# Attention, feed-forward and gated convolution in one kernel: the sign of converted float64 weights by a Prelu slope, and a weight bound from blocks multiplied with themselves

## The chip, the cores and the metric

The kernel runs on one core of a Trainium2 chip. The metric is the device time of one execution in microseconds. TensorE (PE) does matrix products, VectorE (DVE) and ScalarE (ACT) elementwise work and reductions, GpSimd (POOL) almost nothing here, and SyncE's queue (SP) issues every DMA, in order.

## The reference

Three stages follow each other. q and k are rotated by position and attention is computed for 4 batches of 8 heads, 576 positions and 64 features; the result goes through a layer norm, a relu feed-forward with a residual; then through a gated causal convolution over 5 positions.

```python
scores = scale * np.matmul(q_rot, k_rot.transpose(0, 1, 3, 2))
attn = np.exp(scores - max); attn = attn / (sum + 1e-09)
x = np.matmul(attn, v)                       # to (4, 576, 512)
xn = (x - mu) / np.sqrt(var + 1e-06) * g_ln
x = x + np.maximum(xn @ w_ch1, 0.0) @ w_ch2  # 512 -> 2048 -> 512
gate_pre += conv_w[k] * xp[:, k:k + S, :]    # k = 0..4
out = (1 / (1 + np.exp(-gate_pre)) * (x @ w_val)) @ w_out
```

The weights w_ch1 and w_ch2 (512 x 2048 and 2048 x 512), w_val, w_out (512 x 512) and conv_w arrive as float64; the rest is float32.

## The kernel before, in words

[...] A conversion handles 128 x 1024 values of w_ch1 or w_ch2 (eight groups each, w = 0 and 1), or 128 x 512 of w_val and w_out (four groups each), or the 20 columns of conv_w. Its steps are: `load` puts the raw words into one of three buffers in `wall` (w = 0) or one of two buffers `kk` (w = 1); `p1` on ScalarE takes the upper words as float32, once through Abs with a scale of 2^-112 and once through Sign into a float16 scratch; `p2` on VectorE shifts the scaled value left by 3 bits and then ors in the upper bits of the lower word; `p3` on VectorE multiplies by the sign. For w_ch1 and w_ch2 `p3` also sends two matmuls of 512 columns, with the absolute values before the sign is put on, into a PSUM tile `bound`: a sum of all the weights' absolute values by column, with |g_ln| (`gab`) or ones as the stationary side.

When all eight groups of a matrix are in, `conv_scale` reduces `bound` to its maximum and makes a power of two from it (`scl`, and `sg`, which is `scl` times g_ln). With it `conv_hi` (ScalarE) and `conv_lo` (VectorE) split each weight into two float16 halves in `wall`, for which the feed-forward's matmuls (`hp` and `acc`) wait.

This runs beside attention. Work is set into an agenda of slots, one slot for a tile of 128 query rows: scores (`sc`, TensorE), the negative maximum (`nmx`, VectorE), the exponential and a float16 high part (ScalarE), the low part (VectorE), a DMA transpose `pT` and the product with v (`ov`). The conversions of w_ch1 lie two slots apart from slot -7, those of w_ch2 two slots apart from slot 14. The feed-forward begins when the first rows are through attention and the split halves of w_ch1 are there (`w1_ready`), its second layer when those of w_ch2 are (`w2_ready`). The small matrices are converted near the end of attention (`start_tail`).

A scheduler then reorders the instructions of each engine by a timeline of its own, so the order on an engine is not that of the agenda. All loads keep their order among themselves:

```python
with tc.issue_after(last_load[-1]) if last_load else nullcontext():
    last_load.append(nc.sync.dma_start(**kw).ins)
```

A load waits on SP until its buffer is free, and the transposes that come later on SP wait behind it.

Of the kernel before, what the change touches and what calls it, by code (L numbers as in the profile page):

```python
# [7 lines left out]
F32 = mybir.dt.float32  # L8
# [23 lines left out]
def pow2_below_inverse(nc, pool, bound, name):  # L32

    m = pool.tile([128, 1], F32, name=name + "_m", tag=name + "_m", bufs=1)
    nc.vector.tensor_scalar(out=m, in0=bound, scalar1=1e-30, scalar2=1.02, op0=ALU.max, op1=ALU.mult)
    nc.vector.reciprocal(out=m, in_=m)
    r = pool.tile([128, 1], F32, name=name + "_r", tag=name + "_r", bufs=1)
    nc.vector.tensor_scalar(out=r.bitcast(I32), in0=m.bitcast(I32), scalar1=0x7F800000, scalar2=None, op0=ALU.bitwise_and)
    return r


@with_exitstack
def kernel(ctx: ExitStack, tc: tile.TileContext, qk, v, g_ln, w_ch1, w_ch2, w_val, conv_w, w_out, rope, eye, out):
# [69 lines left out]
    w1, w2 = wall[:, 0:16], wall[:, 16:32]  # L113
    wf = wall.rearrange("p u n -> p (u n)").bitcast(F32).rearrange("p (u n) -> p u n", n=512)
    scl = wpool.tile([128, 4], F32, name="scl")
    gab = wpool.tile([128, KD + 1], F32, name="gab")
    sg = wpool.tile([128, KD], F32, name="sg")
    ps_h = L(sF, "ps_h", 1, space=PSUM)
    ps_a = L(sF, "ps_a", 1, space=PSUM)
# [236 lines left out]
    def upper(x):  # L356

        return x.bitcast(BF16).rearrange("p (n two) -> p n two", two=2)[:, :, 1]

    class Conv:  # L360
# [3 lines left out]

        def __init__(self, scratch, src, out, bound=None):
            self.scratch, self.src, self.out, self.bound = scratch, src, out, bound
            self.n = out.shape[1]

        def load(self):
            raw = self.scratch[0][:, 0:2 * self.n].bitcast(I32)
            load_in_order(out=raw.rearrange("p (a n) -> p a n", a=self.src.shape[1]), in_=self.src)
            self.raw = raw.rearrange("p (n two) -> p n two", two=2)

        def p1(self):
            hf = self.raw[:, :, 1].bitcast(F32)
            self.s = self.scratch[1].bitcast(F16)[:, 0:self.n]
            nc.scalar.activation(out=self.out, in_=hf, func=ACTF.Abs, scale=F64_SCALE)
            nc.scalar.activation(out=self.s, in_=hf, func=ACTF.Sign)  # L380

        def p2(self):
            ai = self.out.bitcast(I32)
            nc.vector.tensor_scalar(out=ai, in0=ai, scalar1=3, scalar2=0x7FFFFFFF, op0=ALU.logical_shift_left, op1=ALU.bitwise_and)
            nc.vector.scalar_tensor_tensor(out=ai, in0=self.raw[:, :, 0], scalar=29, in1=ai, op0=ALU.logical_shift_right, op1=ALU.bitwise_or)  # L385

        def p3(self):
            if self.bound is not None:
                o, g, k, last = self.bound
                for j in range(2):  # L390
                    nc.tensor.matmul(o, upper(g).to_broadcast([128, 128]), upper(self.out[:, j * 512:j * 512 + 512]), start=(k == 0 and j == 0), stop=(last and j == 1))
            nc.vector.tensor_tensor(out=self.out, in0=self.out, in1=self.s, op=ALU.mult)

        def schedule(self, i, after=0):
            at(max(i - 3, count[1], after), LD, self.load)
            at(i, AC, self.p1)
            at(i + 1, DV, self.p2)
            at(i + 2, PRE, self.p3)

    wfu = wf.rearrange("p u n -> p (u n)")  # L400
    unit = lambda x, a, n: x[:, a * 512:(a + n) * 512]
    scratch = (
        ([unit(wfu, a, 4) for a in (18, 22, 26)], [unit(wfu, a, 1) for a in (30, 31, 32, 33)]),
        ([unit(k, 0, 4) for k in kk], [unit(wfu, a, 1) for a in (32, 33, 32, 33, 32, 33, 32)] + [unit(kk[0], 0, 1)]),
    )

    def conv_scale(w):
        m = wpool.tile([128, 1], F32, name=f"wm{w}")
        nc.vector.tensor_reduce(out=m, in_=bound[w], axis=AX.X, op=ALU.max)
        r = pow2_below_inverse(nc, wpool, m, f"w{w}")  # L410
        nc.vector.tensor_scalar(out=scl[:, w:w + 1], in0=r, scalar1=2.0 ** 15, scalar2=None, op0=ALU.mult)
        nc.vector.tensor_scalar(out=scl[:, 2 + w:3 + w].bitcast(I32), in0=r.bitcast(I32), scalar1=-1.0, scalar2=float(0x7F000000), op0=ALU.mult, op1=ALU.add)
        if w == 0:
            nc.vector.tensor_scalar(out=sg[:, 0:KD], in0=g_sb, scalar1=scl[:, 0:1], scalar2=None, op0=ALU.mult)
        else:
            nc.vector.tensor_scalar(out=scl[:, 2:3], in0=scl[:, 2:3], scalar1=scl[:, 3:4], scalar2=2.0 ** -30 / (XN_SCALE * H_SCALE), op0=ALU.mult, op1=ALU.mult)
# [14 lines left out]
    def schedule_w(w, a0, step, i):  # L431


        bound[w] = ps_a.tile([128, DM], F32, name=f"bound{w}", tag=f"acc{w}")
        for g in range(8):
            if w == 0:
                fb, c = divmod(g, KD)
                src = w_ch1[c * 128:(c + 1) * 128, fb * 2048:(fb + 1) * 2048].unsqueeze(1)
            else:
                src = w_ch2[g * 256:(g + 1) * 256, :].rearrange("(a p) n -> p a n", p=128)  # L440
            u = 16 * w + 2 * g + 2
            Conv([r[g % len(r)] for r in scratch[w]], src, unit(wfu, u, 2), (bound[w], gab[:, (g % KD if w == 0 else KD):][:, 0:1], g, g == 7)).schedule(int(a0 + g * step), i)
# [131 lines left out]
    def start_tail(i):  # L574
        wp = R(ctx, "w3", 1)
        tw = R(sT, "tw", 1)
        raw = [tw.tile([128, 1024], F32, name=f"r3_{j}") for j in range(4)]
        tmp = [tw.tile([128, 512], F32, name=f"t3_{j}") for j in range(7)]
        rg = (raw, tmp[0:3])
        sc3 = lambda n: [r[n % len(r)] for r in rg]  # L580
        cw = tail["cw"] = wp.tile([128, KT * KD], F32, name="cw")
        Conv(sc3(0), conv_w.unsqueeze(1), cw).schedule(i + 1)
        n = 2
        for nm, src in (("wv", w_val), ("wo", w_out)):
            hi = wp.tile([128, KD, DM], F32R, name=nm + "h")
# [220 lines left out]
```

## Time and profile before

| | |
|---|---|
| median of 3 runs | 808.23 us (802.83 to 810.99) |
| profiled execution | 807.91 us |
| its span, first to last instruction | 805.8 us |
| TensorE busy | 718.7 us, 89% |
| VectorE busy | 628.9 us, 78% |
| ScalarE busy | 499.1 us, 62% |
| mean granted TensorE clock | 0.974 |

The shares are of the whole span; the stages differ, so the rows further down are taken by stretches. An engine's busy time is the time in which one of its instructions runs; neighbours on VectorE and ScalarE overlap by about 0.1 us, so what an instruction costs its queue is read from the starts of two neighbours. The line numbers are those of the kernel before.

### The profile page before, as it was taken

How to read it: one execution, taken by the hardware profiler on the slowest of the kernel's cores; microseconds unless marked ns; L12 is line 12 of the kernel's file. 1: busy time of each engine (PE TensorE's matmuls, PEld its weight loads, DVE VectorE, ACT ScalarE, POOL GpSimd, SP SyncE). 2: the span in 40 equal slices, each digit the busy share in tenths (PEclk: the TensorE clock that was granted, in tenths of full speed). 3: DMA queues.
4: the chain of work that ended last, by engine and by line, in shares of the span. 5: the costliest groups of instructions: out<-in, count | busy, mean ns of one | idle time of the engine just before them, and what ended most of it. 6: DMA issues, size and time to landing. Idle time of an engine off the chain costs nothing.

```text
span 805.8 us, 16042 instructions
## 1 busy us (share of the span) xinstructions
PE 718.7 (89%) x6353; PEld 538.6 (67%) x6360; DVE 628.9 (78%) x1237; ACT 499.1 (62%) x998; POOL 12.5 (2%) x15
## 2 busy tenths in 40 slices
PE   2346757899999988999999999999899999999997
PEld 1124546777776766777776777776567777777996
DVE  5999999999786879677778976655889745547994
ACT  4768777798874766756766767654665333324553
POOL 0000010001000000000000000000000000000000
PEclk9999968899999998999999999999999999999999
DMA  6959776767885776848757855745744102022211
GB/s 241 322 153 279 219 212 177 152 125 163 160 187 92 144 154 122 156 109 141 155 99 150 157 134 95 99 69 97 220 96 79 41 14 53 1 53 52 54 53 53
DMA packets 225835, 103.41 MB, mean 128 GB/s; under 512 B 210528, under 2 KB 213600, under 8 KB 224736
## 3 DMA queue, kind: packets, MB, share of 16 engines
q1 hardware_dynamic: 225760, 102.39, 57.1%
q8 instruction: 50, 0.82, 0.4%
q14 instruction: 25, 0.20, 0.1%
HBM read 45.73 MB, written 4.72 MB: 63 GB/s over the span
## 4 chain that ended last, share of the span: by engine, by line
PE 68%; DVE 14%; DMA 10%; ACT 4%; issue 3%; SPq 1%; ACTq 0%; DVEq 0%
PE acc L548 20%; PE hp L513 20%; PE sc L279 9%; PE pv L649 6%; PE po L666 6%; PE ov L319 4%; DMA raw<-in_qk_dram 3%; DVE nmx L284 2%; PE ov L322 2%; DVE p L298 2%; DMA wall<-in_moe_w_ch_dram 2%; DVE raw L184 2%; DMA kk<-in_moe_w_ch_dram 1%; DMA vt<-in_v_dram 1%; DVE wall L385 1%
## 5 line engine op out<-in xcount | busy, mean ns | idle before, releaser
L513 PE MATMUL hp<-xT,wall 128*128 128x256 f16 (+1 forms) x1920 | 209.4, 266 | 2.9 <-ACT hr L528 1.3
L513 PEld LDWEIGHTS <-wall 128*128 128x128 f16 x1920 | 173.1, 100 | 33.0 <-issue 6.1
L548 PE MATMUL acc<-wall,hh 128*128 128x512 f16 x544 | 162.7, 383 | 5.5 <-DVE t L385 3.1
L291 ACT ACTIVATE p<-sc,nmx 128x576 f32<-128x576 f32 x144 | 106.0, 738 | 69.0 <-DVE nmx L284 67.9
L298 DVE SCALAR_TENSOR_TENSOR p<-p,p 128x576 f16<-128x576 f32 x144 | 107.2, 749 | 24.1 <-ACT p L293 23.5
L284 DVE TENSOR_REDUCE nmx<-sc 128x1 f32<-128x576 f32 x144 | 105.8, 748 | 15.5 <-PE sc L279 15.4
L293 ACT ACTIVATE p<-p 128x576 f16<-128x576 f32 x144 | 96.4, 682 | 18.1 <-DMA pT<-p 16.3
L548 PE MATMUL acc<-wall,hl 128*128 128x512 f16 x272 | 100.5, 381 | 0.2 <-DVE hl L535 0.2
L319 PE MATMUL ov<-vh,pT 128*128 128x64 f16 (+1 forms) x1296 | 95.0, 204 | 4.0 <-ACT vh L235 3.0
L319 PEld LDWEIGHTS <-pT 128*128 128x128 f16 x1296 | 81.4, 103 | 18.2 <-issue 9.8
L548 PEld LDWEIGHTS <-hh 128*128 128x128 f16 x544 | 49.3, 98 | 58.7 <-issue 6.5
L279 PE MATMUL sc<-kq 64*128 64x288 f32 x576 | 82.1, 312 | 5.2 <-ACT p L291 5.2
L535 DVE TENSOR_TENSOR hl<-hr,hh 128x512 f16<-128x512 f32 (+1 forms) x72 | 47.2, 655 | 47.7 <-ACT hr L528 47.6
L526 ACT ACTIVATE hh<-hp 128x512 f16<-128x512 f32 (+1 forms) x72 | 40.8, 567 | 66.5 <-PE hp L513 66.5
L279 PEld LDWEIGHTS sc<-kq 64*128 64x128 f32 x576 | 63.1, 186 | 21.3 <-issue 8.3
L322 PE MATMUL ov<-vl,pT 128*128 128x64 f16 (+1 forms) x720 | 72.7, 204 | 2.3 <-DVE vl L240 2.3
L635 DVE SCALAR_TENSOR_TENSOR gt<-xT,cw,gt 128x256 f32<-128x256 f32 (+12 forms) x192 | 69.6, 412 | 3.3 <-ACT gt L629 2.9
L184 DVE TENSOR_TENSOR raw<-raw,rope_sb 128x1152 f32<-128x1152 f32 (+2 forms) x40 | 44.3, 1111 | 25.1 <-DMA raw<-in_qk_dram 25.1
L322 PEld LDWEIGHTS <-pT 128*128 128x128 f16 x720 | 56.0, 103 | 6.6 <-issue 1.6
L279 PE MATMUL sc<-kx,qs 64*128 64x288 f32 x144 | 34.0, 400 | 24.5 <-ACT p L291 23.5
L666 PE MATMUL po<-woh,gv 128*128 128x512 f32 x144 | 48.7, 403 | 0.0
L279 PEld LDWEIGHTS sc<-kx,qs 64*128 64x128 f32 x144 | 26.8, 259 | 31.8 <-ACT p L291 29.4
(121 smaller groups left out, 1034.8 us busy)
## 6 DMA issues: line engine op xcount, KB each, us to landing
raw<-in_qk_dram SPq DMA_DIRECT2D x28, 576.0 KB, 5.5
wall<-in_moe_w_ch_dram SPq DMA_DIRECT2D x8, 1024.0 KB, 6.5
kk<-in_moe_w_ch_dram SPq DMA_DIRECT2D x8, 1024.0 KB, 6.1
vt<-in_v_dram SPq DMA_DIRECT2D x16, 320.0 KB, 3.7
out_dram<-x SPq DMA_DIRECT2D x18, 256.0 KB, 2.0
pT<-p SPq DMA_TRANSPOSE x144, 3.4
r<-in_moe_w_val_dram SPq DMA_DIRECT2D x4, 512.0 KB, 4.3
r<-in_moe_w_out_dram SPq DMA_DIRECT2D x4, 512.0 KB, 4.5
```

The lines of the kernel that those rows point to most:

```text
L184: nc.vector.tensor_tensor(out=a, in0=a, in1=t, op=ALU.mult)
L279: nc.tensor.matmul(live[i + e][:, half, 0:HS], lw[rows, a], xk[rows, k, half * HS:(half + 1) * HS], start=(n == 0), stop=(n == 2))
L284: nc.vector.tensor_reduce(out=nmx, in_=sc[:, :, 0:HS], axis=AX.XY, op=ALU.max, negate=True)
L291: nc.scalar.activation(out=p32.rearrange("p (e n) -> p e n", e=2), in_=sc[:, :, 0:HS], func=ACTF.Exp, bias=nmx, accum_out=dens[g % 5][:, j ...
L293: nc.scalar.activation(out=p16[:, 0], in_=p32, func=ACTF.Copy, scale=P_SCALE)
L298: nc.vector.scalar_tensor_tensor(out=p16[:, 1], in0=p32, scalar=P_SCALE, in1=p16[:, 0], op0=ALU.mult, op1=ALU.subtract)
L319: nc.tensor.matmul(o, pT[:, c], vh[:, hs, c, :], start=(c == 0), stop=(c == 8))
L322: nc.tensor.matmul(o, pT[:, c], vl[:, hs, c, :], start=False, stop=False)
L513: nc.tensor.matmul(hp[:, j, 0:w], w1[:, u, wl * 512 + o:wl * 512 + o + 128], xT[:, xl * KD + c, 0:w], start=(i == 0), stop=(i == 3 * KD - 1))
L548: tail["last"] = nc.tensor.matmul(st["acc"][s], lw[:, j, sl], w2[:, f + j, lo * 512:lo * 512 + 512], start=(f + j == 0 and i == 0), stop=( ...
L635: nc.vector.scalar_tensor_tensor(out=gt[:, c0:c1], in0=xT[:, c, HALO + c0 - s:HALO + c1 - s], scalar=col(KT - 1 - s), in1=gt[:, c0:c1], op ...
L666: nc.tensor.matmul(po, lw[:, d, sl], rx[:, d, :], start=(n == 0), stop=(n == 3 * KD - 1))
```

## The change

Five things are changed.

- `p1` is one activation, Prelu with the same scale and the slope -(2^32), in place of Abs and Sign. For a negative input the slope makes the result positive and raises its exponent by 32, and the shift by 3 moves that exponent bit into the sign's place. The mask of the shift in `p2` goes, so that its instruction has one operation in place of two.
- `p3` has no product any more. The float16 scratch for the signs goes.
- The bound is taken from the converted weights: for each block of 128 columns, one matmul of the block with itself, all added up in one 128 x 128 tile `bound`. Its largest value is the largest sum of squares by column. A group of 1024 values sends eight such matmuls with a weight load each in place of two of 512 columns.
- `conv_scale` takes the root by halving the exponent (`pow2_below_inverse_root`, one more VectorE instruction than before), and for w_ch1 multiplies by the square of the largest |g_ln| (`gmax`, one more).
- `gmax` is made at the start, by four matmuls of `gab` with the identity and a VectorE reduction.

```diff
+def pow2_below_inverse_root(nc, pool, bound, name):
+    m = pool.tile([128, 1], F32, name=name + "_m", tag=name + "_m", bufs=1)
+    nc.vector.tensor_scalar(out=m, in0=bound, scalar1=1e-30, scalar2=1.05, op0=ALU.max, op1=ALU.mult)
+    nc.vector.reciprocal(out=m, in_=m)
+    r = pool.tile([128, 1], F32, name=name + "_r", tag=name + "_r", bufs=1)
+    nc.vector.tensor_scalar(out=r.bitcast(I32), in0=m.bitcast(I32), scalar1=1, scalar2=0x7F800000, op0=ALU.logical_shift_right, op1=ALU.bitwise_and)
+    nc.vector.tensor_scalar(out=r, in0=r, scalar1=2.0 ** 63, scalar2=None, op0=ALU.mult)
     return r
...
         def p1(self):
-            hf = self.raw[:, :, 1].bitcast(F32)
-            self.s = self.scratch[1].bitcast(F16)[:, 0:self.n]
-            nc.scalar.activation(out=self.out, in_=hf, func=ACTF.Abs, scale=F64_SCALE)
-            nc.scalar.activation(out=self.s, in_=hf, func=ACTF.Sign)
+            nc.scalar.activation(out=self.out, in_=self.raw[:, :, 1].bitcast(F32), func=ACTF.Prelu, scale=F64_SCALE, alpha=-(2.0 ** 32))
 
         def p2(self):
             ai = self.out.bitcast(I32)
-            nc.vector.tensor_scalar(out=ai, in0=ai, scalar1=3, scalar2=0x7FFFFFFF, op0=ALU.logical_shift_left, op1=ALU.bitwise_and)
+            nc.vector.tensor_scalar(out=ai, in0=ai, scalar1=3, scalar2=None, op0=ALU.logical_shift_left)
...
         def p3(self):
-            if self.bound is not None:
-                o, g, k, last = self.bound
-                for j in range(2):
-                    nc.tensor.matmul(o, upper(g).to_broadcast([128, 128]), upper(self.out[:, j * 512:j * 512 + 512]), start=(k == 0 and j == 0), stop=(last and j == 1))
-            nc.vector.tensor_tensor(out=self.out, in0=self.out, in1=self.s, op=ALU.mult)
+            o, start, stop = self.bound
+            k = self.n // 128
+            for j in range(k):
+                x = upper(self.out[:, j * 128:j * 128 + 128])
+                nc.tensor.matmul(o, x, x, start=(start and j == 0), stop=(stop and j == k - 1))
...
         nc.vector.tensor_reduce(out=m, in_=bound[w], axis=AX.X, op=ALU.max)
-        r = pow2_below_inverse(nc, wpool, m, f"w{w}")
+        if w == 0:
+            nc.vector.tensor_scalar(out=m, in0=m, scalar1=gmax, scalar2=gmax, op0=ALU.mult, op1=ALU.mult)
+        r = pow2_below_inverse_root(nc, wpool, m, f"w{w}")
...
-        bound[w] = ps_a.tile([128, DM], F32, name=f"bound{w}", tag=f"acc{w}")
+        bound[w] = ps_a.tile([128, 128], F32, name=f"bound{w}", tag=f"acc{w}")
...
-        tmp = [tw.tile([128, 512], F32, name=f"t3_{j}") for j in range(7)]
+        tmp = [tw.tile([128, 512], F32, name=f"t3_{j}") for j in range(4)]
...
-    nc.vector.memset(gab[:, KD:KD + 1], 1.0)
-    nc.scalar.activation(out=gab[:, 0:KD], in_=g_sb, func=ACTF.Abs)
+    nc.scalar.activation(out=gab, in_=g_sb, func=ACTF.Abs)
+    gt0 = ps_h.tile([128, KD, 128], F32, name="gt0", tag="hp")
+    for c in range(KD):
+        nc.tensor.matmul(gt0[:, c], upper(gab[:, c:c + 1]).to_broadcast([128, 128]), ident, start=True, stop=True)
+    nc.vector.tensor_reduce(out=gmax, in_=gt0, axis=AX.XY, op=ALU.max)
```

In all, VectorE has 22 instructions fewer, ScalarE 25 fewer, TensorE 100 matmuls and 100 weight loads more; the DMAs are the same. The scheduler orders all of it anew. Two places follow.

VectorE in the conversion of w_ch1, around the scale of the first part of v (`vs`, `sv`), in the kernel before. L384 and L385 are the shift and the or of `p2`, L392 is the sign product, L226, L35, L38, L231 and L232 make v's scale, L188 and L206 rotate and split q, L331 belongs to the softmax sum.

```order
L226 TENSOR_REDUCE vm<-hp 128x1
L38 TENSOR_SCALAR vs_r<-vs_m 128x1
L385 SCALAR_TENSOR_TENSOR wall<-wall 128x1024
L188 TENSOR_TENSOR raw<-raw 128x128
L392 TENSOR_TENSOR wall<-wall 128x1024
L231 TENSOR_SCALAR sv<-vs_r 128x1
L232 TENSOR_SCALAR sv<-vs_r 128x1
L35 TENSOR_SCALAR vs_m<-vm 128x1
L384 TENSOR_SCALAR wall<-wall 128x1024
L392 TENSOR_TENSOR wall<-wall 128x1024
L206 SCALAR_TENSOR_TENSOR qs<-raw,qs 128x128
L331 TENSOR_SCALAR rd<-den_63,sv 128x5
```

The same place after the change; L394 and L395 are now the shift and the or, L296 the negative maximum of a score tile, L310 the low part of the probabilities, and lines 196, 243, 244 and 343 are the former 184, 231, 232 and 331.

```order
L394 TENSOR_SCALAR wall<-wall 128x1024
L36 RECIPROCAL vs_m<-vs_m 128x1
L310 SCALAR_TENSOR_TENSOR p_442<-p_440,p_442 128x576
L395 SCALAR_TENSOR_TENSOR wall<-wall 128x1024
L38 TENSOR_SCALAR vs_r<-vs_m 128x1
L296 TENSOR_REDUCE nmx<-sc 128x1 x2
L243 TENSOR_SCALAR sv<-vs_r 128x1
L244 TENSOR_SCALAR sv<-vs_r 128x1
L394 TENSOR_SCALAR wall<-wall 128x1024
L343 TENSOR_SCALAR rd<-den_63,sv 128x5
L196 TENSOR_TENSOR raw<-raw,rope_sb 128x2x128
L395 SCALAR_TENSOR_TENSOR wall<-wall 128x1024
```

Between the scale of v and the first softmax sum there stood two sign products; now only a shift stands there.

SP's queue where the loads of w_ch2 (`kk`) go out, in the kernel before. `raw` is a load of q or k, `pT` the transpose of one tile's probabilities; the numbers behind p are those of its buffers.

```order
L300 DMA_TRANSPOSE pT<-p_603 128x9x128
L66 DMA raw<-in_qk_dram 128x2x320
L66 DMA kk<-in_moe_w_ch_dram 128x2x1024 x2
L66 DMA raw<-in_qk_dram 128x2x320
L300 DMA_TRANSPOSE pT<-p_653 128x9x128
L300 DMA_TRANSPOSE pT<-p_686 128x9x128
L300 DMA_TRANSPOSE pT<-p_727 128x9x128
L66 DMA kk<-in_moe_w_ch_dram 128x2x1024
```

The same place after the change.

```order
L77 DMA kk<-in_moe_w_ch_dram 128x2x1024
L77 DMA raw<-in_qk_dram 128x2x320
L312 DMA_TRANSPOSE pT<-p_603 128x9x128
L312 DMA_TRANSPOSE pT<-p_641 128x9x128
L77 DMA kk<-in_moe_w_ch_dram 128x2x1024
L312 DMA_TRANSPOSE pT<-p_693 128x9x128
L312 DMA_TRANSPOSE pT<-p_726 128x9x128
L77 DMA kk<-in_moe_w_ch_dram 128x2x1024
```

The loads of w_ch2 stood in pairs and then three transposes; now there is one load after every two transposes.

## Rows read from the trace of the kernel before

**Rows 1.** Windows: from, to, busy time of PE, PEld, DVE, ACT, POOL (instructions), clock, DMA, GB/s

```profile
15.00:60.00 45.00, 17.79 (x93) 9.29 (x94) 42.94 (x75) 32.06 (x55) 0.00 (x0) 1.00 0.77 246
60.00:105.00 45.00, 28.59 (x201) 21.99 (x203) 43.88 (x95) 37.21 (x61) 0.00 (x0) 1.00 0.94 252
105.00:165.00 60.00, 45.63 (x510) 40.05 (x514) 57.82 (x94) 44.40 (x90) 4.42 (x2) 0.77 0.73 174
165.00:806.00 641.00, 624.52 (x5543) 465.66 (x5539) 477.73 (x960) 380.30 (x787) 7.56 (x8) 0.99 0.52 105
```

**Rows 2.** Chain of waits from 0 to 200 us, shares of that stretch by line

```profile
by line: PE sc L279 10.6%; issue 6.9%; DMA wall<-in_moe_w_ch_dram 6.8%; PE acc L548 6.5%; PE hp L513 6.0%; DMA kk<-in_moe_w_ch_dram 5.7%; PE ov L319 4.8%; DVE wall L385 4.7%; DVE wall L392 4.2%; DVE raw L184 4.0%; DMA raw<-in_qk_dram 4.0%; 
```

**Rows 3.** Chain of waits, pieces from 92 to 127 us: start, length, what

```profile
93.67 5.73 DMA kk<-in_moe_w_ch_dram
...
102.33 1.02 ACT wall L380
...
122.25 5.09 DMA xT<-x
```

**Rows 4.** Groups by line, whole span: count, busy us, mean ns, idle before and releaser

```profile
L291 ACT ACTIVATE p<-sc,nmx 128x576 f32<-128x576 f32 x144 | 106.0, 738 | 69.0 <-DVE nmx L284 67.9 <-DVE mv L475 0.3 <-DVE vs_r L38 0.2
...
L392 DVE TENSOR_TENSOR wall<-wall 128x1024 f32<-128x1024 f32 x15 | 18.2, 1213 | 0.0
...
L391 PE MATMUL bound<-wall,gab 128*128 128x512 bf16 x25 | 12.9, 590 | 11.0 <-DVE wall L385 11.0
...
L384 DVE TENSOR_SCALAR wall<-wall 128x1024 int32<-128x1024 int32 x16 | 10.9, 681 | 1.0 <-ACT wall L379 0.8
...
L385 DVE SCALAR_TENSOR_TENSOR wall<-wall 128x1024 int32<-128x1024 int32 x8 | 9.7, 1216 | 0.0
...
L379 ACT ACTIVATE wall<-wall 128x1024 f32<-128x1024 f32 x8 | 9.2, 1155 | 6.0 <-DMA wall<-in_moe_w_ch_dram 6.0
...
L379 ACT ACTIVATE wall<-kk 128x1024 f32<-128x1024 f32 x8 | 9.1, 1141 | 4.8 <-DMA kk<-in_moe_w_ch_dram 4.6
...
L380 ACT ACTIVATE wall<-wall 128x1024 f16<-128x1024 f32 x8 | 9.1, 1140 | 0.0
...
L226 DVE TENSOR_REDUCE vm<-hp 128x1 f32<-128x128 f32 x16 | 4.5, 280 | 2.1 <-PE ov L319 1.1 <-PE hp L224 1.0
...
L391 PEld LDWEIGHTS <-gab 128*128 128x128 bf16 x32 | 2.8, 111 | 15.8 <-issue 15.6
...
L409 DVE TENSOR_REDUCE wm<-bound 128x1 f32<-128x512 f32 x2 | 1.4, 680 | 0.0
```

**Rows 5.** VectorE in order of time: start, length, instruction

```profile
98.53 1.21 DVE L392 TENSOR_TENSOR wall<-wall 128x1024 f32<-128x1024 f32 x1
99.66 0.22 DVE L331 TENSOR_SCALAR rd<-den,sv 128x5 f32<-128x5 f32 x1
```

**Rows 6.** TensorE in order of time, merged where equal

```profile
76.64 1.01 PE L391 MATMUL bound<-wall,gab 128*128 128x512 bf16 x2
...
124.12 0.31 PE L322 MATMUL ov<-vl,pT 128*128 128x128 f16 x1
124.23 0.31 PE L319 MATMUL ov<-vh,pT 128*128 128x128 f16 x1
```

**Rows 7.** All engines in order of time from 0 to 8 us

```profile
1.66 0.42 SPq L691 DMA_DIRECT2D ident<-in_eye_dram  x1
...
4.66 0.21 ACT L694 ACTIVATE gab<-g_sb 128x4 f32<-128x4 f32 x1 [2.65 <-DMA g_sb<-in_moe_g_ln_dram]
7.94 1.36 DVE L184 TENSOR_TENSOR raw<-raw,rope_sb 128x1152 f32<-128x1152 f32 x1 [6.91 <-DMA raw<-in_qk_dram]
```

**Rows 8.** DMA issues: KB, median us from issue to landing

```profile
ident<-in_eye_dram SPq DMA_DIRECT2D x1, 32.0 KB, 3.2
```

**Rows 9.** All engines in order of time from 575 to 578 us

```profile
576.11 0.65 ACT L380 ACTIVATE t<-r 128x512 f16<-128x512 f32 x1
...
577.29 1.04 PE L548 MATMUL acc<-wall,hh 128*128 128x512 f16 x4 [3.12 <-DVE t L385]
```

More of the change, by code (lines that the diff above doesn't have):

```diff
@@ L38, in pow2_below_inverse @@
     nc.vector.tensor_scalar(out=r.bitcast(I32), in0=m.bitcast(I32), scalar1=0x7F800000, scalar2=None, op0=ALU.bitwise_and)
+    return r
+def pow2_below_inverse_root(nc, pool, bound, name):
[5 more added lines that the diff above has]
+    nc.vector.tensor_scalar(out=r, in0=r, scalar1=2.0 ** 63, scalar2=None, op0=ALU.mult)
     return r
@@ L115 @@
     scl = wpool.tile([128, 4], F32, name="scl")
-    gab = wpool.tile([128, KD + 1], F32, name="gab")
+    gab = wpool.tile([128, KD], F32, name="gab")
+    gmax = wpool.tile([128, 1], F32, name="gmax")
     sg = wpool.tile([128, KD], F32, name="sg")
@@ L371, in load @@
         def load(self):
-            raw = self.scratch[0][:, 0:2 * self.n].bitcast(I32)
+            raw = self.scratch[:, 0:2 * self.n].bitcast(I32)
             load_in_order(out=raw.rearrange("p (a n) -> p a n", a=self.src.shape[1]), in_=self.src)
@@ L397, in schedule @@
             at(i + 1, DV, self.p2)
-            at(i + 2, PRE, self.p3)
+            if self.bound is not None:
+                at(i + 2, PRE, self.p3)
     wfu = wf.rearrange("p u n -> p (u n)")
@@ L402 @@
     scratch = (
-        ([unit(wfu, a, 4) for a in (18, 22, 26)], [unit(wfu, a, 1) for a in (30, 31, 32, 33)]),
-        ([unit(k, 0, 4) for k in kk], [unit(wfu, a, 1) for a in (32, 33, 32, 33, 32, 33, 32)] + [unit(kk[0], 0, 1)]),
+        [unit(wfu, a, 4) for a in (18, 22, 26)],
+        [unit(k, 0, 4) for k in kk],
     )
@@ L441, in schedule_w @@
             u = 16 * w + 2 * g + 2
-            Conv([r[g % len(r)] for r in scratch[w]], src, unit(wfu, u, 2), (bound[w], gab[:, (g % KD if w == 0 else KD):][:, 0:1], g, g == 7)).schedule(int(a0 + g * step), i)
+            Conv(scratch[w][g % len(scratch[w])], src, unit(wfu, u, 2), (bound[w], g == 0, g == 7)).schedule(int(a0 + g * step), i)
         i = max(i, int(a0 + 7 * step) + 3)
@@ L577, in start_tail @@
         raw = [tw.tile([128, 1024], F32, name=f"r3_{j}") for j in range(4)]
-        tmp = [tw.tile([128, 512], F32, name=f"t3_{j}") for j in range(7)]
-        rg = (raw, tmp[0:3])
-        sc3 = lambda n: [r[n % len(r)] for r in rg]
+        tmp = [tw.tile([128, 512], F32, name=f"t3_{j}") for j in range(4)]
+        sc3 = lambda n: raw[n % 4]
         cw = tail["cw"] = wp.tile([128, KT * KD], F32, name="cw")
@@ L588, in start_tail @@
             for c in range(KD):
-                t = tmp[3 + n % 4]
+                t = tmp[n % 4]
                 Conv(sc3(n - 1), src[c * 128:(c + 1) * 128, :].unsqueeze(1), t).schedule(i + n)
```

## The prediction

> **What bounds the kernel now.** I read the busy time by stretches first [rows 1], because the share of a whole span mixes stages with different limits. The reader should see two regimes. From 165 us to the end TensorE is the limit: 624.5 of 641 us busy, 16.5 idle. From 15 to 165 us it is VectorE: 42.9 + 43.9 + 57.8 = 144.6 of 150 us, while TensorE is busy for 92.0 and idle for 58, and ScalarE is busy for 113.7. The weights are converted in exactly these 150 us. All later matmuls queue behind that stretch at nearly full rate, so a microsecond taken out of it should arrive at the end, and one taken from VectorE or ScalarE after 165 us should not.
>
> The chain of waits [rows 2] is the second view, because a busy engine is not yet what everything waits for. Over the first 200 us the sign product holds 4.2% of the chain, 8.4 us, against some 18 us that it costs VectorE. The other products lie where the chain takes another way, most of all from 92 to 127 us: a weight load that was behind a transpose on SP's queue (93.67 us, 5.73 us long), ScalarE converting it with exponentials queued behind, TensorE getting its scores late, and at 122.25 us the transposed activations of the first layer [rows 3]. VectorE is just as full there, but relieving it alone moves nothing on that path while the order stays.
>
> **The change part by part.** *The sign product.* There are 16 for the two large matrices, 1213 ns each [rows 4]; the next instruction starts 1.13 us after one starts (98.53 to 99.66) [rows 5], so VectorE's queue loses 16 x 1.13 = 18.1 us. All lie inside the VectorE stretch. If VectorE alone decided, the end would move by all of it.
>
> *The Sign on ScalarE.* 16 activations go, each of which holds the queue for 1.02 us (the piece at 102.33) [rows 3], 16 us in all. ScalarE has 36 us idle there, so I count only what stood on the chain where it passes VectorE by: that one piece, 1.0 us.
>
> *Prelu for Abs.* No row shows a Prelu. Abs took 1155 and 1141 ns and Sign 1140 on the same 1024 elements [rows 4]; I take the same, since two functions already agree. The upper end is the dearest row by element, the exponential with 738 ns for 576 elements: 1.31 us, so 16 x 0.16 = 2.6 us on ScalarE, in its idle time. From below there is nothing under Sign's 1140 ns, a gain of 0.
>
> The Trainium skill says (ScalarE activation tables: per-element evaluation and per-set limits, What a function is on this engine) that with the same operands an activation costs the same whichever function's table it reads; no run here shows that for Prelu.
>
> *The shift with one operation in place of two.* Its row is 681 ns [rows 4], and I keep that. The far end is the 1216 ns of the other integer row of this width: 0.53 x 16 = 8.5 us back on VectorE. Fewer operations on the same operands speak against it, so it only widens the range.
>
> *The bound.* Before, a group sent two matmuls of 512 columns; after, eight of 128: 1024 columns each time, but eight weight loads instead of two. The two took 1.01 us (76.64) [rows 6]. The 128-column matmuls of the same stage, each with its own weight load, start 0.11 us apart (124.12, 124.23) [rows 6], so eight take 0.9 us, and I take 0 for the edit. The other end is that six more loads of 0.111 us [rows 4] show in full: 0.67 us a group, 10.7 us for 16, in a stretch where TensorE has 58 us idle.
>
> The Trainium skill speaks for that other end (TensorE: Matmul & The Clock Gate, Part 3: Packing small matmuls — row/col tiling): a weight load overlaps matmuls in flight only when it goes to another row group, and these use all rows. By that rule the sum below would be 803 instead of 793 if all of it delayed scores. The trace does not agree: the matmuls at 124 us use all rows too and are 0.11 us apart, the length of their columns alone.
>
> *Around it.* The reduction of a bound shrinks from 512 to 128 columns, 680 to 280 ns by the like reduction of vm [rows 4], twice, 0.8 us less. Three tiny instructions come on VectorE, which I let stand against that. They lengthen the way from the bound to the first scaled weights by two places, and the new order puts more work between; those weights are still ahead of the activations that need them, because everything in front is shorter. At the start the maximum of g takes four small matmuls and a reduction of 0.68 us. gab is there at 4.87 us and the identity at 1.66 + 3.2 = 4.86 us, and VectorE waits until 7.94 anyway [rows 7, 8], so it ends near 6.3 us: cost 0, and 0.7 us once if that cover were gone.
>
> *The small weights at 570 us.* Eight products and nine Signs go from a stretch that TensorE limits. One place counts: at 577.29 TensorE had waited 3.12 us for a relu that sat on ScalarE behind a Sign begun at 576.11 [rows 9], which held the queue for 0.55 us. I count 0.5 us.
>
> *The order.* The scheduler writes all queues anew. On VectorE shift and or pairs remain with attention work between them; on SP the second matrix's loads go out one at a time between transposes instead of in pairs. The first layer's matmuls still begin among the same score tiles (22 done, against 24), so TensorE's work behind the stretch stays what it was.
>
> **The sum.** 18.1 us on VectorE, less the four products that start from 98 to 118 us, where the chain passes VectorE by (4 x 1.13 = 4.5), plus 1.0 for the Sign there and 0.5 for the late stretch: 15.1 us. The profiled execution took 807.9 us (span 805.8 and 2.1 around it), 0.3 below the median of the runs, so both give the same: 807.9 - 15.1 = 792.8, **793 us**.
>
> **Rivals.**
>
> *The load chain decides more of the stretch.* Then only the products on the chain count: 8.4 + 1.0 + 0.5 = 9.9, which gives 798. For it: the DMA engines were busy for 0.77 x 45 + 0.94 x 45 + 0.73 x 60 = 121 of the 150 us [rows 1], and that must fit into some 135. Against it: the loads are spread on SP now, and two of the three steps in that chain are ScalarE's and TensorE's queues, of which the first gets shorter too.
>
> *The bound's weight loads show.* 10.7 us are given back if all of it delays scores: 803. Against it stands the row at 124 us.
>
> *More than VectorE's share.* From 105 to 165 us TensorE was granted 0.77 of full speed [rows 1], about 28 us at the lower level. At the stage's busy share, 0.76, that is 21 us of matmuls, which would take 10.6 at the upper level. If denser work keeps the upper level and two thirds of that reach the path, 7 us come on top of 18.1 + 0.5: 782.
>
> *ScalarE waits at the head of its queue for the loads: no gain, or slower.* Abs waits for its load in order, with exponentials behind it: 6.0 + 4.6 us [rows 4], 0.66 us for each of the 16 loads. With a faster VectorE ScalarE comes to that place sooner, but a load takes 5.73 us to land [rows 3] however fast VectorE is. If the mean wait grows by 1.13 us, to 1.8, the whole gain is eaten: 807. From 2.3 us on the kernel is over 1% slower; a mean of 2.8 gives 824. For it: DMA at 0.94 from 60 to 105 us. Against: a load is issued when its buffer comes free, which is VectorE's doing, so it comes sooner too.
>
> *It does not do what it says.* Prelu could have brought a table load each time; the new order has two table loads in all, as before, so I give it nothing.
>
> **How the numbers follow.** Forecast (gain 12 to 19 us) 0.56; load chain 0.19; more than VectorE's share 0.11; the bound's loads 0.03; loads at ScalarE's head 0.11, of which 0.06 near 807 and 0.05 slower. About 1%, 8 us, is what a measurement of this kernel tells from no change, since its three runs spread from 802.8 to 811.0. Faster by that: 0.56 + 0.11 + 0.16 of the load chain = 0.83. Within 1%: 0.03 of the load chain + 0.03 + 0.06 = 0.12. Slower: 0.05. The range goes from 782, the clock's case, to 801, which takes in the load chain and the upper end of the shift in part; it leaves out the cases at 803 and above and the tails.
>
> **What would show it.** In the profile after, TensorE's full stretch should begin at about 150 us instead of 165; VectorE should be over 90% busy before it; a bound group should take about 0.9 us, a Prelu 1.14 us; the maximum of g should be done before 7.9 us; and the full stretch should be as long as before, 641 us, within 3. I am wrong if VectorE stands idle for weight loads before 150 us (the load chain), if bound groups take 1.5 us, or if TensorE's full stretch itself changes its length.

## Result and profile after

| | before | after |
|---|---|---|
| median | 808.37 us (802.83 to 810.99, 4 runs) | 788.35 us (785.88 to 790.89, 4 runs) |
| profiled execution, its span | 807.91, 805.8 us | 790.89, 789.1 us |
| TensorE busy, idle within the span | 718.7, 87.1 us | 720.3, 68.8 us |

The ratio is 0.976, with an interval from 0.972 to 0.979: 20 us by the medians, 17.0 by the two profiled executions (that of after is the slowest of its four).

The windows of after (from:to, length, busy time and count of PE, PEld, DVE, ACT, POOL, granted clock, DMA share, GB/s) answer to [rows 1]; the third stretch of before is cut at 150 us here.

```profile
15.00:60.00 45.00, 23.50 (x178) 17.95 (x178) 40.20 (x80) 30.20 (x56) 0.00 (x0) 1.00 0.99 278
60.00:105.00 45.00, 32.75 (x301) 28.53 (x302) 44.40 (x98) 35.75 (x66) 0.56 (x1) 0.89 1.05 267
105.00:150.00 45.00, 35.65 (x461) 32.11 (x458) 44.23 (x76) 35.90 (x75) 1.54 (x1) 0.89 0.94 188
150.00:165.00 15.00, 15.00 (x163) 10.63 (x163) 13.34 (x24) 13.68 (x27) 0.00 (x0) 1.00 0.56 100
165.00:789.00 624.00, 610.66 (x5354) 455.59 (x5350) 457.84 (x924) 359.99 (x745) 5.91 (x8) 0.98 0.52 105
```

Length less PE busy gives TensorE's idle time. From 15 to 165 us it was 58.0 and is 43.1, 14.9 less; after 165 us it was 16.5 and is 13.3; before 15 us it is 0.6 less. TensorE's busy time did not fall (720.3 against 718.7 us), so what was gained between the two profiles is idle time. From 150 to 165 us TensorE is busy throughout, where before it was not full until 165 us. The DMA engines have a busy share of 0.99 and 1.05 in the first two stretches, where before they had 0.77 and 0.94.

The groups by line of after (instruction, shape, count | busy us, mean ns | idle before, and what ended it) answer to [rows 4].

```profile
L390 ACT ACTIVATE wall<-kk 128x1024 f32<-128x1024 f32 x8 | 9.1, 1143 | 7.1 <-DMA kk<-in_moe_w_ch_dram 7.0
L390 ACT ACTIVATE wall<-wall 128x1024 f32<-128x1024 f32 x8 | 9.1, 1139 | 9.0 <-DMA wall<-in_moe_w_ch_dram 9.0
...
L394 DVE TENSOR_SCALAR wall<-wall 128x1024 int32<-128x1024 int32 x16 | 11.0, 690 | 4.0 <-ACT wall L390 4.0
L395 DVE SCALAR_TENSOR_TENSOR wall<-wall 128x1024 int32<-128x1024 int32 x8 | 9.8, 1220 | 0.0
...
L402 PEld LDWEIGHTS <-wall 128*128 128x128 bf16 x128 | 11.2, 129 | 11.6 <-DVE wall L395 9.6 <-issue 1.3 <-DVE p L310 0.3
```

A Prelu takes 1139 and 1143 ns, an Abs took 1155 and 1141; the shift with one operation takes 690 ns, with two it took 681.

TensorE in order of time, one group of the bound, and VectorE at the start (start, length, instruction, idle before it):

```profile
17.24 1.03 PE L402 MATMUL bound<-wall 128*128 128x128 bf16 x8 [3.95 <-DVE wall L395]
```

```profile
5.97 0.69 DVE L710 TENSOR_REDUCE gmax<-gt 128x1 f32<-128x512 f32 x1 [4.95 <-PE gt L709]
7.41 1.70 DVE L196 TENSOR_TENSOR raw<-raw,rope_sb 128x1152 f32<-128x1152 f32 x2 [0.75 <-DMA raw<-in_qk_dram]
```

Eight matmuls with eight weight loads take 1.03 us, about what the two of 512 columns with two loads took (1.01) [rows 6], and the maximum of g ends 0.75 us before VectorE has anything else to do.

What [rows 3] showed of before, the path over a load, ScalarE and TensorE from 92 to 127 us, is gone. The chain of waits of after from 80 to 130 us, shares by line:

```profile
by line: issue 15.1%; DVE nmx L296 14.0%; DVE wall L395 14.0%; DVE p L310 12.5%; DVE wall L440 12.5%; DVE raw L196 8.5%; DVE wall L394 6.0%; DVE raw L200 3.7%; DVE qs L218 2.3%; DVE x L355 2.2%; DVE bs L486 2.0%; DVE kq L218 1.8%; DVE x L54
```

Apart from issue, time in which the engine waited for nothing that the profile shows, every piece named there is VectorE's. I had forecast that the path would stay and had taken four products off the sum for it. That the total came out nearly right did not show that its terms were right, so they were tested one by one.

### The profile page after: what moved, and what is told of

Same layout as the page of the kernel before. It is cut to its first block, busy times and chain, and to the rows that moved or that the text cites. A ratio compares the mean times of both kernels' runs of the same rounds, so it can differ in the third digit from the quotient of the medians.

```text
span 789.1 us, 16180 instructions
## 1 busy us (share of the span) xinstructions
PE 720.3 (91%) x6460; PEld 546.6 (69%) x6460; DVE 607.7 (77%) x1215; ACT 479.6 (61%) x973; POOL 8.5 (1%) x15
## 4 chain that ended last, share of the span: by engine, by line
PE 69%; DVE 13%; DMA 11%; issue 3%; ACT 3%; SPq 1%; ACTq 0%; DVEq 0%
PE acc L561 21%; PE hp L526 20%; PE sc L291 9%; PE pv L661 6%; PE po L678 6%; DMA raw<-in_qk_dram 4%; PE ov L331 4%; DMA pT<-p 3%; DVE nmx L296 2%; DVE p L310 2%; DVE raw L196 2%; PE ov L334 2%; DMA kk<-in_moe_w_ch_dram 2%; DVE wall L395 1%; DMA wall<-in_moe_w_ch_dram 1%
## 5 line engine op out<-in xcount | busy, mean ns | idle before, releaser
L310 DVE SCALAR_TENSOR_TENSOR p<-p,p 128x576 f16<-128x576 f32 x144 | 107.9, 754 | 24.0 <-ACT p L305 23.3
L296 DVE TENSOR_REDUCE nmx<-sc 128x1 f32<-128x576 f32 x144 | 106.6, 754 | 14.2 <-PE sc L291 14.2
L331 PE MATMUL ov<-vh,pT 128*128 128x64 f16 (+1 forms) x1296 | 92.3, 202 | 3.1 <-DMA pT<-p 2.7
L331 PEld LDWEIGHTS <-pT 128*128 128x128 f16 x1296 | 78.9, 102 | 18.4 <-issue 9.3
L291 PE MATMUL sc<-kq 64*128 64x288 f32 x576 | 84.3, 316 | 2.7 <-ACT p L303 2.7
L291 PEld LDWEIGHTS sc<-kq 64*128 64x128 f32 x576 | 64.9, 189 | 18.4 <-issue 7.9
L334 PEld LDWEIGHTS <-pT 128*128 128x128 f16 x720 | 54.8, 102 | 6.1 <-issue 1.8
L196 DVE TENSOR_TENSOR raw<-raw,rope_sb 128x1152 f32<-128x1152 f32 (+2 forms) x40 | 44.5, 1115 | 13.6 <-DMA raw<-in_qk_dram 13.5
L291 PE MATMUL sc<-kx,qs 64*128 64x288 f32 x144 | 33.0, 390 | 18.1 <-ACT p L303 18.1
L561 PEld LDWEIGHTS <-hl 128*128 128x128 f16 x272 | 26.1, 99 | 27.7 <-issue 2.2
```

The costliest lines, as they stand in the source:

```text
L196: nc.vector.tensor_tensor(out=a, in0=a, in1=t, op=ALU.mult)
L291: nc.tensor.matmul(live[i + e][:, half, 0:HS], lw[rows, a], xk[rows, k, half * HS:(half + 1) * HS], start=(n == 0), stop=(n == 2))
L296: nc.vector.tensor_reduce(out=nmx, in_=sc[:, :, 0:HS], axis=AX.XY, op=ALU.max, negate=True)
L310: nc.vector.scalar_tensor_tensor(out=p16[:, 1], in0=p32, scalar=P_SCALE, in1=p16[:, 0], op0=ALU.mult, op1=ALU.subtract)
L331: nc.tensor.matmul(o, pT[:, c], vh[:, hs, c, :], start=(c == 0), stop=(c == 8))
L334: nc.tensor.matmul(o, pT[:, c], vl[:, hs, c, :], start=False, stop=False)
```

## Experiments

Three theories at first. **Queue:** VectorE's queue decides, the product is the whole gain, and a Sign costs nothing. **Chain:** the path over loads, ScalarE and TensorE decides in part, so a Sign costs up to 10 us. **Order:** the gain comes from the rewritten order of the queues. Every kernel below changes the kernel after, unless it says otherwise. The kernel before was timed again with each of the three groups of runs (medians 809.1, 807.8 and 808.9 us), the kernel after only at first, so the third column compares across groups.

| kernel | median, us | to after (788.4) | ratio to before, interval |
|---|---|---|---|
| Prelu part undone, new bound kept | 810.8 | +22.5 | 1.003, 1.000 to 1.005 |
| unread Sign, 16 groups | 798.0 | +9.6 | 0.987, 0.982 to 0.992 |
| product, 16 groups | 812.4 | +24.1 | 1.005, 1.002 to 1.007 |
| the product's instruction, one column wide | 791.5 | +3.1 | 0.979, 0.975 to 0.984 |
| product, w_ch1 only | 801.7 | +13.3 | 0.993, 0.990 to 0.995 |
| product, w_ch2 only | 796.2 | +7.8 | 0.986, 0.984 to 0.989 |
| unread Sign, w_ch1 only | 798.0 | +9.6 | 0.989, 0.984 to 0.993 |
| unread Sign, 7 groups of w_ch2 | 791.1 | +2.7 | 0.981, 0.978 to 0.983 |
| no or of the low words | 779.4 | -8.9 | 0.962, 0.958 to 0.967 |
| all weight loads on GpSimd's queue | 799.5 | +11.2 | 0.988, 0.984 to 0.992 |
| v's loads on GpSimd's queue | 811.7 | +23.3 | 1.003, 1.000 to 1.006 |
| before, v's loads on GpSimd's queue | 814.6 | (before: +5.7) | 1.007, 1.004 to 1.010 |

**The bound alone.** Abs, Sign, mask and product are back as before; the bound, its scale and the maximum of g stay as after.

```diff
-            nc.scalar.activation(out=self.out, in_=self.raw[:, :, 1].bitcast(F32), func=ACTF.Prelu, scale=F64_SCALE, alpha=-(2.0 ** 32))
+            nc.scalar.activation(out=self.out, in_=hf, func=ACTF.Abs, scale=F64_SCALE)
+            nc.scalar.activation(out=self.s, in_=hf, func=ACTF.Sign)
...
+            nc.vector.tensor_tensor(out=self.out, in0=self.out, in1=self.s, op=ALU.mult)
```

> The changed kernel with its Prelu part undone: Abs, Sign, the mask and the sign product stand as in the kernel before, and only the bound from blocks with themselves stays. Queue theory (VectorE's queue is the limit from 15 to 150 us, so what it saves arrives at the end and nothing else does): 806 to 809 us, since the bound costs TensorE nothing that shows and VectorE loses only 0.6 us. Chain theory (the chain of waits of the kernel before decides: loads, ScalarE, TensorE): also 806 to 810. Order theory (a good part of the 20 us comes from a luckier order or from the new bound): clearly below 804.

810.8 us, 2 us above the queue theory's range: none of the gain is left. The bound alone, with the order that goes with it, brings nothing; the gain comes with the Prelu part and the order that goes with that.

**The Sign put back, unread.**

```diff
             nc.scalar.activation(out=self.out, in_=self.raw[:, :, 1].bitcast(F32), func=ACTF.Prelu, scale=F64_SCALE, alpha=-(2.0 ** 32))
+            if self.bound is not None:
+                nc.scalar.activation(out=self.sgn, in_=self.raw[:, :, 1].bitcast(F32), func=ACTF.Sign)
```

> The changed kernel with ScalarE's Sign put back for the 16 groups of the two large matrices, written into the scratch of before, where nothing reads it. Queue theory: ScalarE has room, 788 to 791 us. Chain theory (ScalarE with loads at the head of its queue is on the path): several us come back, 793 to 800. Order theory: anything within 5 us of 788.

798.0 us, the chain theory's range. The chain of waits of this kernel, from 80 to 130 us, runs over the path that after no longer has (L392 is the Sign of a w_ch2 group):

```profile
81.38 6.21 DMA kk<-in_moe_w_ch_dram
87.63 1.00 issue
88.63 1.11 ACT wall L392
89.75 0.73 ACT p L303 x2
90.48 0.04 issue
90.52 3.15 PE sc L291 x11
...
95.29 0.84 SPq L312
...
96.23 6.28 DMA kk<-in_moe_w_ch_dram
```

A weight load lands, ScalarE converts it (the Prelu in the piece called issue, then the Sign) before it gets to two exponentials, TensorE has its scores late, the next transpose waits on SP, and the next load goes out behind it. Whether the Signs in this chain are what costs the 9.6 us is asked further down, one matrix at a time.

**The product put back, without any Sign.**

```diff
+            nc.vector.tensor_tensor(out=self.out, in0=self.out, in1=self.out, op=ALU.max)
```

> The changed kernel with one more VectorE operation for each of the 16 groups, 1024 wide as the sign product was (the maximum of the converted weights with themselves), no Sign. Queue theory: 16 x 1.13 = 18 us come back, 804 to 808. Chain theory: only the products that stood on the chain of before come back, 8 us, so 795 to 798. Order theory: less than 5 us, below 794.

812.4 us, 4 us above the queue theory's range: the gain is gone although ScalarE has no Sign. Together with the last runs: without the product the Signs cost 9.6 us, with it nothing (812.4 without them, 810.8 with them). The two parts do not add up.

**The same instruction on one column,** for what its place in the order and its waits cost without its time.

```diff
+            nc.vector.tensor_tensor(out=self.out[:, 0:1], in0=self.out[:, 0:1], in1=self.out[:, 0:1], op=ALU.max)
```

> A control for the one before: the same operation at the same place, but one column wide, so that the order and the wait for the bound's matmuls change and the work does not. Queue and chain theory: 788 to 791 us. If it lies more than 4 us away, the order that the scheduler happens to find is worth that much, and differences of that size between kernels mean nothing.

791.5 us: about 3 us of the rows above may be order alone. A difference below that is not read by itself.

**Where it costs.** The product on one matrix at a time (`if self.w == 0`, `if self.w == 1`), then the Sign on one at a time.

> The changed kernel, with a VectorE operation of the product's size (maximum of a value with itself) on the eight groups of w_ch1 alone. Changed kernel 788.4; all 16 such operations gave 812.4, 24 more. Queue theory, now in its second form (each product costs its 1.13 us of VectorE, and above that something which only comes when products stand in both matrices): 8 x 1.13 = 9 more, 797. Two-limits theory (VectorE's queue alone rules up to about 80 us, where w_ch1 is converted; the load chain stands just under it from 80 to 117 us): a product costs its full 1.13 us here, 796 to 799, and the excess over 18 us that the 16 showed is not here. Delay-grows theory (a product early in the stretch lets TensorE's clock fall and moves all later loads): more than 12, over 800.

> The same with the eight groups of w_ch2 alone. Queue theory: 9 more, 797. Two-limits theory: the product holds the buffer and VectorE's queue between 80 and 130 us, where the load chain is close behind, so each costs its 1.13 us and some of the next load's landing as well: 12 to 15 more, 800 to 803, and with the eight of w_ch1 together the 24 that all 16 showed. If the load chain had cover to spare there, the products would cost less than 9: under 796.

> The changed kernel, with a ScalarE Sign that nothing reads on the eight groups of w_ch1 alone. All 16 gave 798.0, 9.6 more. Two-limits theory: up to 80 us VectorE rules and ScalarE has idle time, so nothing to 2 us: 788 to 790. ScalarE-share theory (every Sign costs the same wherever it stands): 8 x 0.6 = 4.8 more, 793.

> The same Sign on the first seven groups of w_ch2 alone, none of them written into the first transpose buffer (in the run with all 16, one was). Two-limits theory: here ScalarE's conversion is a piece of the load chain (load, conversion with exponentials behind it, scores on TensorE, transpose, next load), so nearly all of the 9.6 us comes back: 795 to 799. ScalarE-share theory: 7 x 0.6 = 4.2 more, 792.6. If it was the buffer held longer by the one Sign written there, nothing: 788 to 790.

My second theory, two limits in two places, had the places the wrong way round. Both the product (+13.3 against +7.8) and the Sign (+9.6 against +2.7) cost most on w_ch1, in the first half of the stretch. So the Signs of w_ch2 in the chain shown above are not what cost the 9.6 us: on w_ch2 alone they cost less than the 3 us that order may make.

With products on w_ch2 alone VectorE is busy for 89.5 of 90 us in the two windows from 60 to 150 us, and 8 x 1.13 = 9.0 us of work cost 7.8, within 3 us of its full price.

```profile
60.00:105.00 45.00, 30.96 (x279) 27.08 (x280) 44.50 (x95) 34.25 (x60) 1.00 (x1) 0.88 1.00 256
105.00:150.00 45.00, 34.06 (x389) 29.70 (x387) 45.00 (x69) 30.88 (x64) 0.56 (x1) 0.78 0.73 162
```

With products on w_ch1 alone they cost 4.3 us more than VectorE's time. VectorE in order of time, just ahead of the low part of v (`vl`):

```profile
45.58 1.22 DVE L404 TENSOR_TENSOR wall<-wall 128x1024 f32<-128x1024 f32 x1
...
51.68 1.22 DVE L404 TENSOR_TENSOR wall<-wall 128x1024 f32<-128x1024 f32 x1
52.81 0.88 DVE L252 SCALAR_TENSOR_TENSOR vl<-vt,sv,vh 128x640 f16<-128x640 f32 x1
```

and SP's queue of the same kernel (start, time on the queue, transfer):

```profile
39.34 0.33 SPq L77 DMA_DIRECT2D wall<-in_moe_w_ch_dram  x1
53.72 0.33 SPq L77 DMA_DIRECT2D vt<-in_v_dram  x1
...
54.58 0.46 SPq L77 DMA_DIRECT2D wall<-in_moe_w_ch_dram  x1
...
70.09 0.65 SPq L77 DMA_DIRECT2D kk<-in_moe_w_ch_dram  x1
```

In the kernel after, the same places:

```profile
44.12 0.89 DVE L252 SCALAR_TENSOR_TENSOR vl<-vt,sv,vh 128x640 f16<-128x640 f32 x1
```

```profile
45.04 0.33 SPq L77 DMA_DIRECT2D vt<-in_v_dram  x1
...
45.89 0.59 SPq L77 DMA_DIRECT2D wall<-in_moe_w_ch_dram  x1
...
58.06 0.46 SPq L77 DMA_DIRECT2D kk<-in_moe_w_ch_dram  x1
59.44 1.85 SPq L312 DMA_TRANSPOSE pT<-p  x1
61.34 0.79 SPq L77 DMA_DIRECT2D kk<-in_moe_w_ch_dram  x1
```

A load of v needs the buffer that this `vl` frees (the waits below name its neighbours `vs_r` and `vs_m` in VectorE's queue), so SP stands still from 39.7 to 53.7 us, and the eighth weight load goes out 8.7 us later than in after (54.58, 45.89), the ninth 12.0 later (70.09, 58.06). The kernel before stood there too, for 14.1 us (SP's waits from 38 to 62 us: releaser, total, times, longest), after for 4.4:

```profile
SPq L66 <- DVE vs_r L38: 14.1, 1, 14.1
```

```profile
SPq L77 <- DVE vs_m L36: 4.4, 1, 4.4
```

The busy share of the DMA engines from 45 to 60 us differs accordingly, before, with products on w_ch1, and after: 0.39, 0.55, 1.00.

```profile
45.00:60.00 15.00, 6.29 (x47) 3.77 (x46) 13.09 (x30) 9.93 (x18) 0.00 (x0) 1.00 0.39 104
```

```profile
45.00:60.00 15.00, 6.98 (x70) 5.56 (x71) 13.35 (x34) 9.23 (x18) 0.00 (x0) 1.00 0.55 131
```

```profile
45.00:60.00 15.00, 9.71 (x91) 7.46 (x89) 10.80 (x28) 9.59 (x17) 0.00 (x0) 1.00 1.00 211
```

The late loads are not shown to be the whole of the 13.3 us. 801.7 us lies in the range of the delay-grows theory (over 800), and no run took that theory apart. The first lines of the two pages, with products on w_ch1 and after (busy time, share of the span and count), give the same 6460 matmuls:

```profile
PE 726.7 (91%) x6460; PEld 555.7 (69%) x6460; DVE 616.9 (77%) x1223; ACT 479.8 (60%) x973; POOL 11.8 (1%) x15
```

```profile
PE 720.3 (91%) x6460; PEld 546.6 (69%) x6460; DVE 607.7 (77%) x1215; ACT 479.6 (61%) x973; POOL 8.5 (1%) x15
```

Of the 12.2 us between these two spans (801.3 and 789.1), 6.4 are longer busy time of TensorE and 5.8 are idle time. Its granted clock was 0.79 from 105 to 150 us and 0.73 from there to 165, where after had 0.89 and 1.00. With all 16 products TensorE's busy time was 720.0 us and all of the loss was idle time, so the clock does not explain the products' price in general.

With a Sign on w_ch1 the place is the tenth load, as in the run with all 16 Signs (68.37). SP of the kernel with w_ch1's Signs:

```profile
60.86 0.49 SPq L77 DMA_DIRECT2D kk<-in_moe_w_ch_dram  x1
61.45 7.95 SPq L312 DMA_TRANSPOSE pT<-p  x3
69.45 1.43 SPq L77 DMA_DIRECT2D kk<-in_moe_w_ch_dram  x1
```

Three transposes stand between two loads, where after has one, and the tenth load goes at 69.45 instead of 61.34. The scheduler put them there when the Signs came in, so this run does not separate ScalarE's time from the new order; that stays open.

**Is it SP's wait for v?** If so, v's loads on another queue should give the 9 us back.

```diff
-            load_in_order(out=st["vt"], in_=v[b, pr])
+            nc.gpsimd.dma_start(out=st["vt"], in_=v[b, pr])
```

> The kernel before (products and Signs in it), with the loads of v issued on GpSimd's queue instead of SP's; nothing is left out. In the kernel before a load of v stood in SP's queue from 40.0 to 54.1 us, waiting 14.1 us for VectorE to come to it, and the eighth weight load went out behind it at 54.9, against 45.9 in the changed kernel. SP-queue theory (a product on VectorE costs so much because SP's queue waits for VectorE's place in the queue and the weight loads stand behind that wait): the eighth load goes some 9 us earlier, and 5 to 10 us of it arrive at the end, 798 to 803. VectorE-queue theory (VectorE's own full queue decides, whatever the loads do): within 2 us of the kernel before, 808. Rival against both: vectors of v that come sooner push weight loads aside on the DMA engines, 810 or more.

> The same on the changed kernel. There the load of v waited 4.4 us, and the DMA engines did not run dry behind it (1.00 from 45 to 60 us, against 0.39 before). SP-queue theory: little is left to gain, 784 to 788, so the difference between the two kernels shrinks from 20 us to about 15. VectorE-queue theory: 788, and the difference stays at 20.

Neither the SP-queue theory's times nor the VectorE-queue theory's came. The kernel before went to 814.6 us, in the range of the rival (810 or more), but its profile does not bear out loads pushed aside: TensorE is idle for 85.6 us, 1.5 less than before, and busy for 724.2, 5.5 more, at a granted clock of 0.942 against 0.974. The eighth load goes 6.5 us sooner, but the ninth and tenth do not:

```profile
48.42 0.33 SPq L66 DMA_DIRECT2D wall<-in_moe_w_ch_dram  x1
48.79 0.43 SPq L66 DMA_DIRECT2D raw<-in_qk_dram  x1
49.34 6.34 SPq L300 DMA_TRANSPOSE pT<-p  x2
58.67 0.38 SPq L66 DMA_DIRECT2D raw<-in_qk_dram  x1
62.37 3.09 SPq L300 DMA_TRANSPOSE pT<-p  x2
...
66.14 1.00 SPq L66 DMA_DIRECT2D kk<-in_moe_w_ch_dram  x2
```

SP now waits for VectorE at the transposes (`p`, 6.9 us in three waits from 38 to 68 us) and at other loads, and the two loads go at 66.1, against 65.4 before. Taking this one wait off SP did not bring the later loads forward; VectorE's lateness shows at whichever entry comes next. On the kernel after, the last weight load goes at 106.3 us as without the edit and TensorE is busy for as long up to 165 us (109.7 us in both), so the time was lost later. Of the 18.7 us between the two spans 11.2 are idle time and 7.5 longer busy time of TensorE. The idle time from 165 to 345 us is 13.6 us instead of 3.9, and the layer norm's powers on GpSimd now stand among v's loads that wait for buffers. That this is why the time went was not tested. What SP's waits cost as a whole stays open.

**All weight loads on GpSimd's queue.**

```diff
-            load_in_order(out=raw.rearrange("p (a n) -> p a n", a=self.src.shape[1]), in_=self.src)
+            go = load_in_order if self.bound is None else nc.gpsimd.dma_start
+            go(out=raw.rearrange("p (a n) -> p a n", a=self.src.shape[1]), in_=self.src)
```

> The changed kernel with all 16 weight loads on GpSimd's queue, so that none stands behind a transpose or a load of v; nothing is left out. SP-queue theory: loads wait only for their own buffers, and what SP's queue cost in the changed kernel (kk loads that stand behind transposes) comes back: 778 to 786. VectorE-queue theory: 788. Rival: weight loads and first loads of q and k now compete, and transposes take longer, 790 to 800.

799.5 us, the rival's range. Its chain of waits begins with

```profile
3.09 17.82 DMA raw<-in_qk_dram
```

where the like piece of after is

```profile
2.13 5.18 DMA raw<-in_qk_dram
```

Five weight loads now share the DMA engines with the first load of q and k, and TensorE is idle for 40.2 of the first 60 us, against 33.7.

**Less for VectorE still.**

```diff
-            nc.vector.scalar_tensor_tensor(out=ai, in0=self.raw[:, :, 0], scalar=29, in1=ai, op0=ALU.logical_shift_right, op1=ALU.bitwise_or)
```

> The changed kernel without the or of the low words (the lowest three mantissa bits of all converted weights are left out): 16 more VectorE operations of 1.22 us go from the stretch. It asks what rules the changed kernel. VectorE-queue theory: 15 to 19 us less again, 769 to 773. SP-queue theory with the loads now close to what the DMA engines can carry (busy 1.0 from 45 to 120 us): 3 to 8 less, 780 to 785.

779.4 us: of some 18 us less on VectorE's queue in the stretch (16 x 1.13), 8.9 arrive, under what pure queue theory gave and just beyond the loads' range. Had VectorE alone been the limit of the kernel after, nearly all would have come. The edit does more than take time off VectorE: the or is the last reader of the raw words, so without it a load's buffer comes free after the Prelu, and the 8.9 us do not price VectorE alone. It leaves out bits of the weights, so it is no kernel to use, and no kernel here beats the one after with the whole computation.

## Why the prediction came out, step by step

The forecast was 793 us in a range from 782 to 801; 788.4 was measured, a gain of 20.0 us by the medians where the sum had 15.1. Where the gain lay was right: 14.9 us of TensorE's idle time went from the stretch between 15 and 165 us, where the sum had 18.1 - 4.5 + 1.0 = 14.6. That these two agree so closely is partly luck, since the profiled execution of after is the slowest of its four. How the sum was put together was not right.

*The product, 18.1 less 4.5.* Put back alone it costs 24.1 us, about 21 if the one-column run's 3 us are taken for order. The step that failed is the discount, four products "where the chain passes VectorE by". It held the path of [rows 3] fixed. On w_ch2, where those four are, eight cost 7.8 of their 9.0 us; with the discount they would have cost 4.5. On w_ch1 eight cost 13.3, 4.3 more than their own time. Up to 3 us of that may be order; weight loads left SP later there and TensorE's matmuls took longer, and which of these cost how much stays open.

*The Sign, 1.0.* Undersized, but only once the product is gone: 9.6 us then, 0 with it. I read one piece off a chain of before, in which I take VectorE to have been the later of two nearly equal paths over most of the stretch. Which part of the 9.6 is ScalarE's time and which the new order of the transposes is not shown. A chain names one path; it does not say how far behind the next one is.

*The load chain as a rival, 798.* It was set against the forecast as one or the other. The run with the Sign kept and the product gone, 798.0, has that chain from 80 to 130 us; the change removed a piece of each path and so got past both. That its time equals the rival's is chance: the rival counted the products on the chain and one Sign. With the product taken first, 12.8 us belong to it (810.8 to 798.0) and 9.6 to the Sign; with the Sign first, nothing to the Sign and all to the product.

*The late stretch, 0.5.* The wait of 3.12 us [rows 9] is 0.55 us shorter in after:

```profile
558.93 1.89 PE L561 MATMUL acc<-wall,hh 128*128 128x512 f16 x4 [2.57 <-ACT hh L539]
```

TensorE idles for 3 us less after 165 us in all, while it is busy for 1.6 us more over the span; no run split that up.

*More than VectorE's share, 782.* The granted clock did rise, from 0.77 to 0.89 between 105 and 150 us and to 1.00 between 150 and 165, but TensorE's busy time did not fall, so no gain of that kind shows.

*ScalarE at the head of its queue, 807 or slower.* Its waits for weight loads did grow, from 10.6 us [rows 4] to 16.0, from 0.66 to 1.0 us a load, and did not eat the gain.

*What was put at nothing.* Prelu, the shift, the bound and the maximum of g came out as forecast, in the rows above and in the run with the bound alone. The Trainium skill's sentence that an activation costs the same whichever function's table it reads (ScalarE activation tables: per-element evaluation and per-set limits, What a function is on this engine) agrees with 1139 and 1143 ns for the Prelu and 1155 and 1141 for the Abs. The Trainium skill's rule that a weight load overlaps matmuls only in another row group (TensorE: Matmul & The Clock Gate, Part 3: Packing small matmuls — row/col tiling) does not agree as it stands, though the same section also lets a load into the background weight buffer go ahead of matmuls in flight: all 128 rows are used, a load takes 129 ns, and eight loads with their eight matmuls are done in 1.03 us, where 1024 columns with two loads took 1.01.

*What would show it.* TensorE is full from 150 us, and from there to the end it is 639 us, within the 3 us of 641; a group of the bound takes 1.03 us instead of 0.9. VectorE was to be over 90% busy: it is in the second and third stretch (44.4 and 44.2 of 45) but not quite in the first (40.2), where the DMA engines' share is now 0.99. The sign of the load chain showed in part: VectorE's idle time before a shift, ended by ScalarE's step before it, grew from 0.8 to 4.0 us in all.

## What to carry to other kernels

Where two paths are nearly as long, take off the chain's pieces one at a time on paper and ask which path is then the longest: a part that is worth nothing alone, as the Sign was, can be worth half of the whole together with another, and the gains of single parts do not add up. Where an in-order DMA queue waits for buffers that a late engine frees, look at when the loads go out and not only at the engine's busy time; how much the late loads cost here is not settled. Moving loads to another queue did not help in any of the three runs that tried it.

## What the runs showed of the hardware

Transfers issued on GpSimd's queue took longer to land than the same ones on SP's when they were moved there: a w_ch1 load 8.6 us against 6.9 and a w_ch2 load 7.8 against 5.9 (medians of eight), in another order and with more transfers at once.

The granted clock shown for a stretch need not be the one that its matmuls had. From 45 to 75 us the kernel after shows 1.00, the upper of the two levels, and the one without the or 0.50, the lower, yet six score matmuls in a row take 1.80 us and a group of the bound 1.04 us in both, and TensorE's busy time for a like number of matmuls is about the same:

```profile
45.00:75.00 30.00, 21.03 (x179) 17.22 (x177) 25.55 (x73) 22.44 (x41) 0.00 (x0) 1.00 1.05 250
```

```profile
45.00:75.00 30.00, 21.31 (x191) 18.01 (x191) 27.07 (x74) 26.92 (x47) 0.00 (x0) 0.50 1.10 256
```

A group of the bound took 1.03 us at 17 us and 0.63 us at 126 us of the kernel after, so in early stretches durations say more than the granted clock.
